# A gated long convolution and a token mixer on one core: the first channel chunk's inverse transform set aside, its gate moved behind the second chunk's spectrum stage, and the early loads reordered

## The chip, the core and the metric

The kernel runs on one core of a Trainium2 chip, in float32 (the large matrix products split each operand into a rounded half and a rest). The metric is device time in microseconds of one execution. Timed executions give a median; one further execution, taken by the hardware profiler, gives the trace that is read here.

## What is computed

Cut to what matters (S = 2048 tokens, D = 640 channels, F = 1728):

```python
sa, ca, ga, sb, cb, gb = six rows of  silu(c) @ w_mod          # (640,) @ (640, 3840)
x  = q
h  = layernorm(x) * (1 + ca) + sa
kv = causal_conv4(k, shift_k) * v                               # 4 taps, per channel
y  = causal_conv_2048(kv, ssm_k) + kv * ssm_D                   # per channel, by FFT of length 4096
x  = x + ga * (h * y)
h  = layernorm(x) * (1 + cb) + sb
x  = x + gb * (gelu(h^T @ w1 + b1) @ w2 + b2)^T                 # MLP over the token axis
```

## The kernel before

The order of all work is written by hand: each engine runs its instructions in program order, and a wait stands only where data or a buffer needs it. SyncE issues nearly all DMAs, also in program order, so a load whose destination is still in use holds up every load behind it.

The 640 channels are cut into NC = 5 chunks of DC = 128. For each chunk the long convolution runs as a transform in stages:

- `kv_ops(g)`, g = 0 to 3: the four-tap convolution and the product with v, for a quarter of the tokens, eight elementwise operations; on VectorE (one operand of the products lies in PSUM) or, with other scratch (`T_t`), on GpSimd. The result goes to X. k lies in the front and v in the rear of `T_in` (KX, VX), both chunk by chunk in the same place.
- `perm(c)`: ScalarE reorders ssm_k of the chunk from `T_aux` into P, after `perm_add(c)` has added ssm_D to its first tap. P also holds the products of the spectrum stage.
- `step1(side, t)`: first forward step (L218), side 0 from X, side 1 from P; four parts of 32 matmuls, each evicted by ScalarE (L220) into Z.
- `f2(g)`, g = 0 to 7: the spectrum stage, 64 matmuls (L233), a ScalarE copy (L237) into `T_kt`, two VectorE multiplies into P, and two sums into Y, which GpSimd does one stage later (VectorE for the last).
- `i2(r)`, r = 0, 1: first inverse step (L262), two PSUM tiles, four ScalarE evictions (L271) over the second half of Z.
- `i1(half)`: second inverse step (L282), with the constant v1, which lies in `T_v1`.
- `a1_ops(c)`: `ac`, 16 ScalarE operations (L289) that normalise the rows of q for the chunk's channels into A1 (in `T_aux`), and `po`, VectorE operations that apply the modulation rows G1 and G0.
- `gate(c, ps, half)`: VectorE multiplies A1 by the result in PSUM, GpSimd adds it to x; `spill(c)` writes x to memory.

PSUM tiles come from a ring of three (`psum()`); a fourth tile (`tap`) holds the taps and scratch of the convolution.

Before the chunk loop, chunk 0 is loaded and convolved, both its forward steps run, chunk 1 is convolved for the greater part, and q, then four of the five parts of the first half of w_mod are loaded. In chunk c's turn the stages f2 (with the rest of the convolution as `fill`, a few operations per stage), step1(0) of chunk c+1, i2, i1, gate and step1(1) of chunk c+1 follow. Chunk 0's turn is special: between these it also takes the statistics of q (L542, L543), the modulation rows (`mod_part`, L342; `mod_sum`; `mod_row`, L353) and the root of the layernorm; the parts of w_mod lie in `T_v1`, `T_aux` and P, which is why the constant v1 and ssm_k of chunk 1 are loaded only after the parts have been used:

```python
            for kk in range(4):
                mod_part(tap, kk, pl[kk])
                if kk == 1:
                    sync.dma_start(T_v1[:, 0:4096], c_v1, max_dma_last_dim=4096)
                if kk == 2:
                    load_ks(1)
            rstd(rs1, nm1, 0, 16)
```

After the five turns the token MLP follows, with large matmuls (L436, L997, L1074) that TensorE paces.

Of the kernel before, what the change touches and what calls it, by code (L numbers as in the profile page):

```python
# [12 lines left out]
ALU = mybir.AluOpType  # L13
# [36 lines left out]
def mixer_kernel(ctx: ExitStack, tc: tile.TileContext, q, k, v, shift_k, ssm_k, ssm_D, w1, b1, w2, b2, c,  # L50
# [235 lines left out]
    def a1_ops(c):  # L286

        g = lambda G: G[:, None, c * DC:(c + 1) * DC].to_broadcast([128, 16, DC])
        ac = [lambda j=j: act.activation(A1[:, j], XR(j, DC * c, DC), AF.Identity, scale=rs1[:, j:j + 1],  # L289
                                         bias=nm1[:, j:j + 1]) for j in range(16)]  # L290
        po = [lambda: TT(dve, A1, A1, g(G1), ALU.mult), lambda: TT(dve, A1, A1, g(G0), ALU.add)]
        if c in (0, NC - 1):
# [162 lines left out]
    load_ks(0, act)  # L455

# [21 lines left out]
    sync.dma_start(stg[0:13, :], dram(b1, 0, [[128, 13], [1, 128]]))  # L478
    sync.dma_start(stg[13:14, :].rearrange("p (h m) -> p h m", h=2), dram(b1, 1664, [[64, 1], [0, 2], [1, 64]]))
    sync.dma_start(stg[14:30, :], dram(b2, 0, [[128, 16], [1, 128]]))  # L480
    sync.dma_start(stg[30:35, :], dram(c, 0, [[128, 5], [1, 128]]))
# [3 lines left out]
    load_taps(2)  # L485
# [13 lines left out]
    pl = [three(t) for t in (T_v1, T_v1[:, 1920:3840], T_aux, T_aux[:, 2048:3968], P)]  # L499

    for kk in range(4):
        mod_load(0, kk, (T_v1[:, 0:1920], T_v1[:, 1920:3840], T_aux[:, 0:1920], T_aux[:, 2048:3968])[kk])
# [8 lines left out]
    for c in range(NC):  # L511
# [3 lines left out]
        for g in range(8):  # L515
# [17 lines left out]
            if c and cn is not None and g == 3:  # L533
                perm_add(cn)
# [4 lines left out]
        if c == 0:  # L539
            for j in range(16):  # L540
                for h in range(2):
                    dve.bn_stats(bst[:, j, h, :], XR(j, 320 * h, 320))  # L542
                dve.bn_aggr(mv[:, j, :], bst[:, j, 0:2, :])  # L543
        if c and c + 2 < NC:
            taps()
            if c + 3 < NC:
                load_taps(c + 3)
        if c == 0:
            mod_load(0, 4, P[:, 0:1920])
            for t in range(4):  # L550
                step1(0, t)
            ps = psum()
            pe.transpose(ps[:, 0:36], stg, ID[0:36, 0:36])
            act.activation(cols, ps[:, 0:36], AF.Copy)
            act.activation(sil, cols[:, 30:35], AF.Silu)
            i2(0)
            for kk in range(4):
                mod_part(tap, kk, pl[kk])
                if kk == 1:
                    sync.dma_start(T_v1[:, 0:4096], c_v1, max_dma_last_dim=4096)  # L560
                if kk == 2:
                    load_ks(1)
            rstd(rs1, nm1, 0, 16)
            run(ac[0:4])
            i2(1)
            mod_part(tap, 4, pl[4])
            load_k(2, 1)
            load_k(2, 2)
            load_v(2, 2)
            load_halo(2)  # L570
            load_k(2, 0)
            load_v(2, 0)
            load_v(2, 1)
            load_k(2, 3)
            load_v(2, 3)
            mod_sum(tap, T_kt[:, 0:640])
            run(ac[4:8])
            pool.tensor_scalar(PW, TR.rearrange("p (i s) -> p s i", s=4), 1.0, None, op0=ALU.mult)
            run(kv_ops(2, pool))
            for i in range(3):  # L580
                mod_row(i, T_kt[:, 0:640])
            taps()
            load_taps(3)
            perm_add(1, dve)
            perm(1)
            load_ks(2)
            run(ac[8:16])
            run(po[0:2])
            fill.extend(kv(3, ((0,), (1, 2), (3,))))
# [46 lines left out]
        for half in range(2):  # L636
            ps = i1(half)
            if c and half:
                dv(3)
            elif c:  # L640
                k0 = step1(1, 0, True)
            elif half:
                run(po[2:4])
            gate(c, ps, half)
        spill(c)
        if c:
            k0()
        for t in range(1 if c else 0, 4):
            step1(1, t)
# [3 lines left out]
        else:  # L653
            dv(11 if c else 8)
# [483 lines left out]
```

## Time and profile before

| what | value |
|---|---|
| median of three timed runs | 700.2 us (699.32 to 700.36) |
| profiled execution | 697.86 us, its span from the first to the last instruction 696.1 us |
| mean granted TensorE clock | 0.975 |
| first `f2` matmul of chunks 0, 1, 2, 3, 4 | 40.8, 115.4, 164.9, 209.2, 257.4 us |
| q | 32 loads of 160 KB, issued from 41.2 to about 68.9 us |
| w_mod, first half | 5 loads of 960 KB, issued from 68.9 to 72.5 us |
| constant v1; ssm_k of chunk 1 | 2048 KB, issued at 79.4 us; 2 loads of 512 KB, issued from 81.2 us |
| k and v, per chunk | 8 loads of 128 KB each, in packets of 256 bytes |

All numbers of the profile come from the one profiled execution. A row of the timeline reads: start, time, engine, line, operation, output and inputs, count, and in brackets the idle time ahead of it with what ended it. A row of the windows reads: stretch, length, busy time and instructions of each engine, granted clock, share of the DMA engines' time, GB/s. L59 is a helper through which all two-operand elementwise operations go, so those are told apart by their tiles.

### The profile page before, as it was taken

How to read it: one execution, taken by the hardware profiler on the slowest of the kernel's cores; microseconds unless marked ns; L12 is line 12 of the kernel's file. 1: busy time of each engine (PE TensorE's matmuls, PEld its weight loads, DVE VectorE, ACT ScalarE, POOL GpSimd, SP SyncE). 2: the span in 40 equal slices, each digit the busy share in tenths (PEclk: the TensorE clock that was granted, in tenths of full speed). 3: DMA queues.
4: the chain of work that ended last, by engine and by line, in shares of the span. 5: the costliest groups of instructions: out<-in, count | busy, mean ns of one | idle time of the engine just before them, and what ended most of it. 6: DMA issues, size and time to landing. Idle time of an engine off the chain costs nothing.

```text
span 696.1 us, 20691 instructions
## 1 busy us (share of the span) xinstructions
PE 622.0 (89%) x9099; PEld 595.8 (86%) x9099; DVE 496.1 (71%) x866; ACT 291.6 (42%) x464; POOL 128.2 (18%) x147
## 2 busy tenths in 40 slices
PE   0689777898998988888899999999999989999997
PEld 0688466788988888778899979999999989999997
DVE  6769448978979449888985741123499868888986
ACT  0444373554746536456666232232244233233331
POOL 5184018513425025000100000000000430000000
PEclk9999798999999999999999999999999999999999
DMA  9988988627443424171305604433353533466611
GB/s 183 243 227 232 381 169 178 145 43 155 91 79 111 145 64 121 59 153 32 60 1 91 121 2 99 84 61 64 110 141 104 167 121 99 121 173 172 167 44 38
DMA packets 166930, 84.37 MB, mean 121 GB/s; under 512 B 91030, under 2 KB 157368, under 8 KB 166840
## 3 DMA queue, kind: packets, MB, share of 16 engines
q1 hardware_dynamic: 162292, 81.74, 46.9%
q10 hardware_dynamic: 4548, 1.31, 1.1%
q8 instruction: 71, 1.16, 0.7%
q14 instruction: 19, 0.16, 0.1%
HBM read 72.55 MB, written 10.49 MB: 119 GB/s over the span
## 4 chain that ended last, share of the span: by engine, by line
PE 62%; DVE 17%; DMA 6%; ACT 5%; SPq 4%; issue 3%; POOL 1%; ACTq 0%; POOLq 0%; DVEq 0%
PE pst L436 20%; PE pst L997 17%; PE pst L1074 7%; PE pst L218 5%; PE pst L233 4%; PE pst L262 4%; SPq L496 3%; DVE tap L59 3%; PE pst L282 2%; DVE p L59 2%; DMA aux<-in_A_ssm_k_dram 2%; DVE kt L59 2%; DMA w<-in_const_w_dram 1%; DMA aux<-in_w_mod_dram 1%; DVE aux L59 1%
## 5 line engine op out<-in xcount | busy, mean ns | idle before, releaser
L233 PE MATMUL pst<-z,w 128*64 128x64 f32 x2560 | 79.0, 223 | 12.0 <-ACT z L220 5.7
L233 PEld LDWEIGHTS pst<-z,w 128*64 128x64 f32 x2560 | 76.8, 138 | 14.8 <-issue 7.7
L220 ACT ACTIVATE z<-pst 128x1024 f32<-128x1024 f32 x40 | 43.0, 1076 | 51.4 <-PE pst L218 51.3
L218 PE MATMUL pst<-v,x 128*64 128x128 f32 x640 | 39.6, 282 | 27.2 <-DVE x L59 24.1
L218 PEld LDWEIGHTS pst<-v,x 128*64 128x64 f32 x640 | 36.9, 142 | 28.1 <-POOL t L459 23.6
L59 DVE TENSOR_TENSOR p<-pst,kt 128x512 f32<-128x512 f32 x80 | 50.9, 680 | 12.7 <-ACT kt L237 9.3
L59 POOL TENSOR_TENSOR y<-p 128x256 f32<-128x256 f32 x72 | 51.1, 744 | 38.8 <-DVE p L59 38.6
L218 PE MATMUL pst<-v,p 128*64 128x128 f32 x640 | 39.7, 283 | 6.8 <-DVE aux L59 4.6
L997 PE MATMUL pst<-r_z,m_w 128*128 128x320 f32 x222 | 42.1, 312 | 2.2 <-DVE m_w L59 2.2
L218 PEld LDWEIGHTS pst<-v,p 128*64 128x64 f32 x640 | 37.2, 143 | 8.0 <-DVE aux L59 4.9
L262 PEld LDWEIGHTS pst<-v,y 32*128 32x128 f32 x1280 | 39.7, 194 | 3.8 <-issue 2.6
L237 ACT ACTIVATE kt<-pst 128x512 f32<-128x512 f32 x40 | 23.9, 599 | 43.7 <-PE pst L233 30.1
L262 PE MATMUL pst<-v,y 32*128 32x64 f32 x1280 | 41.6, 279 | 0.7 <-ACT z L220 0.6
L833 ACT ACTIVATE pst<-pst,sm 128x640 f32<-128x640 f32 x13 | 10.0, 767 | 75.8 <-PE pst L436 75.8
L985 ACT ACTIVATE m_w<-m_v 128x896 fp32r<-128x896 f32 x24 | 22.7, 951 | 37.0 <-PE pst L997 16.8
L997 PEld LDWEIGHTS pst<-r_z,m_w 128*128 128x128 f32 x222 | 35.2, 190 | 2.4 <-DVE m_w L59 2.4
L59 DVE TENSOR_TENSOR tap<-tap,kt 128x512 f32<-128x512 f32 x51 | 35.5, 696 | 1.3
L59 DVE TENSOR_TENSOR kt<-in,tap 128x512 f32<-128x512 f32 x51 | 34.9, 685 | 1.4
L59 POOL TENSOR_TENSOR m_p<-u_i,r_z 128x320 f32<-128x320 f32 x1 | 0.9, 882 | 183.4 <-issue 183.4
L271 ACT ACTIVATE z<-pst 128x512 f32<-128x512 f32 x38 | 20.9, 646 | 21.9 <-PE pst L262 21.9
L59 DVE TENSOR_TENSOR m_w<-m_v,m_w 128x896 fp32r<-128x896 f32 x24 | 27.9, 1164 | 2.4 <-ACT m_w L985 1.9
L436 PE MATMUL pst<-r_z,wb0b 128*128 128x320 f32 x180 | 28.2, 310 | 0.9 <-DVE u_x L59 0.9
(289 smaller groups left out, 1445.0 us busy)
## 6 DMA issues: line engine op xcount, KB each, us to landing
x<-in_B_w_dram SPq DMA_DIRECT2D x20, 512.0 KB
aux<-in_A_ssm_k_dram SPq DMA_DIRECT2D x10, 512.0 KB
in<-in_A_k_dram SPq DMA_DIRECT2D x36, 128.0 KB
in<-in_A_v_dram SPq DMA_DIRECT2D x36, 128.0 KB
m_x<-xs SPq DMA_DIRECT2D x28, 160.0 KB
out_dram<-m_x SPq DMA_DIRECT2D x28, 160.0 KB
w<-in_const_w_dram SPq DMA_DIRECT2D x2, 2048.0 KB
m_v<-in_B_w_dram SPq DMA_DIRECT2D x9, 448.0 KB
```

The costliest lines, as they stand in the source:

```text
L59: TT = lambda eng, o, a, b, op: eng.tensor_tensor(o, a, b, op=op)
L218: pe.matmul(ps[64 * ri:64 * ri + 64, o:o + 255:2], lhs, F1[:, 128 * ri:128 * ri + 128], start=True, stop=True)
L220: evac = lambda: act.activation(Z[:, side, t], ps.rearrange("p (a k e) -> p a k e", a=4, e=2), AF.Copy)
L233: pe.matmul(ps[64 * h:64 * h + 64, o:o + 64], W2[k1 // 32][:, 2 * (k1 % 32) + ri], rhs, start=True, stop=True)
L237: act.activation(kt.rearrange("p (m i) -> p m i", i=32), pv[:, :, 1], AF.Copy)
L262: pe.matmul(pp[qd // 2][:, o:o + 64], Y[p, ri, i:i + 2].rearrange("p i k -> p (i k)"), V2[p, 64 * ri:64 * ri + 64], start=ri == 0, stop=ri ...
L271: act.activation(o, i, AF.Copy)
L436: pe.matmul(ps[0:m, h, 0:320], w_.bitcast(F32R), r_[:, 320 * h:320 * h + 320].bitcast(F32R), start=first and i == 0, stop=last and i == 2)
L496: sync.dma_start(XH[j // 8][64 * b:64 * b + 64, j % 8], dram(q, (16 * b + j) * D, [[32 * D, 64], [1, D]]))
L985: act.activation(W[n][0].bitcast(F32R), A[p, w_], AF.Copy)
L997: pe.matmul(bank[n], w[:, i].bitcast(F32R), r.bitcast(F32R), start=i == 0 and k == 0, stop=i == 6 and k == 2)
L1074: pe.matmul(acc[s][:, h, 0:320], w[:, f_].bitcast(F32R), u[r + h].bitcast(F32R), start=f_ == 0 and k == 0, stop=f_ == NF - 1 and k == 2)
```

## The change

Chunk 0 is no longer gated in its own turn. The results of its `i1` are copied by ScalarE into `Y0`, which lies in v's place, and the turn of chunk 1 does the gate in four quarters (`late(n)`, rows 4n to 4n+3): the normalising of quarters 0 and 1 in the first stages of chunk 1's spectrum stage, their VectorE operations behind its end, quarters 2 and 3 among the inverse steps. The statistics of q are spread likewise: rows 0 to 7 in chunk 0's turn, 8 to 11 in chunk 1's spectrum stage, 12 to 15 behind it, with the roots by quarters (`q_root`, `q_newton`).

So that v's place is free, chunk 2 is convolved whole in chunk 0's turn; chunk 3 follows at the end of chunk 1's turn, a quarter on GpSimd and 24 operations on VectorE, 16 of them left for chunk 2's spectrum stage, spread over eight stages instead of six. Chunk 0's and 1's turns leave the common path by `continue`; those of chunks 2 to 4 keep it.

The loads stand in another order on SyncE: behind the constants of the spectrum stage ssm_k of chunk 1 and the taps of chunk 2, the constant v1, k and v of chunk 2, the first half of w_mod (now into the place of q, `T_x`), and then q, in 16 loads of two rows instead of 32 of one, which waits for the modulation's matmuls. The four small loads of b1, b2 and c go to ScalarE's queue.

The diff, cut to its core:

```diff
@@ prologue
     load_ks(0, act)
+    act.dma_start(stg[0:13, :], dram(b1, 0, [[128, 13], [1, 128]]))
...
-    load_taps(2)
...
-    for j in range(16):
-        for b in range(2):
-            sync.dma_start(XH[j // 8][64 * b:64 * b + 64, j % 8], dram(q, (16 * b + j) * D, [[32 * D, 64], [1, D]]))
+    def load_q():
+        for j in range(0, 16, 2):
+            for b in range(2):
+                sync.dma_start(XH[j // 8][64 * b:64 * b + 64, j % 8:j % 8 + 2],
+                               dram(q, (16 * b + j) * D, [[32 * D, 64], [D, 2], [1, D]]))
+    def q_stats(js):
+        for j in js:
+            for h in range(2):
+                dve.bn_stats(bst[:, j, h, :], XR(j, 320 * h, 320))
+            dve.bn_aggr(mv[:, j, :], bst[:, j, 0:2, :])
...
+    def q_root(n):
+        act.activation(tm[:, 4 * n:4 * n + 4], mv[:, 4 * n:4 * n + 4, 1], AF.Sqrt)
+    def q_newton(n):
+        o = slice(4 * n, 4 * n + 4)
+        newton(rs1[:, o], tm[:, o], mv[:, o, 1])
+        dve.scalar_tensor_tensor(nm1[:, o], mv[:, o, 0], -1.0, rs1[:, o], op0=ALU.mult, op1=ALU.mult)
+    Y0 = T_in[:, 2240:4288].rearrange("p (j d) -> p j d", j=16)
+    def late(n):
+        t = ((T_t, T_kt)[n // 2])[:, 512 * (n % 2):512 * (n % 2) + 512].rearrange("p (j d) -> p j d", j=4)
...
+        return ac, [lambda: TT(dve, t, t, g(G1), ALU.mult), lambda: TT(dve, t, t, g(G0), ALU.add),
+                    lambda: TT(dve, t, t, Y0[:, 4 * n:4 * n + 4], ALU.mult), lambda: TT(pool, x, x, t, ALU.add)]
...
+    load_ks(1)
+    load_taps(2)
+    sync.dma_start(T_v1[:, 0:4096], c_v1, max_dma_last_dim=4096)
...
@@ spectrum stage
-            if c:
+            if c > 1:
                 for f_ in ac[2 * g:2 * g + 2]:
                     f_()
+            if c == 1 and g < 2:
+                run(late(g)[0])
+            if c == 1 and g < 4:
+                q_stats(range(8 + g, 9 + g))
+            if c == 1 and 3 < g < 6:
+                run(ac[4 * g - 16:4 * g - 12])
+            if c == 1 and g == 4:
+                q_root(2)
+            if c == 1 and g == 5:
+                q_newton(2)
...
-            dv(-(-len(fill) // max((6 if c else 8) - g, 1)))
+            dv(-(-len(fill) // max((6 if c > 2 else 8) - g, 1)))
@@ chunk 0's turn, new
+            load_halo(2)
+            for g in range(4):
+                load_k(2, g)
+                load_v(2, g)
+            for kk in range(4):
+                mod_load(0, kk, T_x[kk // 2][:, 1920 * (kk % 2):1920 * (kk % 2) + 1920])
...
+            perm_add(1)
+            perm(1)
+            taps()
...
+            for t in range(4):
                 step1(0, t)
+            run(kv_ops(1, pool))
+            for g in (0, 2, 3):
+                run(kv_ops(g))
+            i2(0)
+            i2(1)
+            for half in range(2):
+                ps = i1(half)
+                act.activation(Y0[:, 8 * half:8 * half + 8].rearrange("p j (y e c) -> p e (j y) c", e=2, c=2),
+                               ps.rearrange("p (e y c) -> p e y c", e=2, c=2), AF.Copy)
+            ps = psum()
+            for kk in range(5):
+                mod_part(ps, kk, pl[kk])
+            load_q()
+            load_ks(2)
...
+            mod_sum(ps, T_kt[:, 0:640])
+            q_stats(range(4))
+            for t in range(4):
+                step1(1, t)
+                if t < 3:
+                    mod_row(t, T_kt[:, 0:640])
+            q_stats(range(4, 8))
+            for n in range(2):
+                q_root(n)
+                q_newton(n)
+            continue
@@ chunk 1's turn, new
+            run(late(0)[1] + late(1)[1])
+            q_stats(range(12, 16))
+            run(late(2)[0] + ac[8:12])
+            step1(0, 0)
+            step1(0, 1)
+            run(late(2)[1])
             i2(0)
+            q_root(3)
+            q_newton(3)
+            run(late(3)[0])
+            step1(0, 2)
+            run(late(3)[1])
             i2(1)
+            run(ac[12:16])
+            step1(0, 3)
+            run(po)
...
+            spill(0)
+            perm_add(2)
+            perm(2)
...
+            for half in range(2):
+                ps = i1(half)
+                gate(1, ps, half)
+            spill(1)
+            for t in range(4):
+                step1(1, t)
+            run(kv_ops(2, pool))
+            fill.extend(kv(4, ((0,), (1, 2), (3,))))
+            dv(8)
+            continue
```

More of the change, by code (lines that the diff above doesn't have):

```diff
@@ L531, in mixer_kernel @@
                                    dram(w1, (16 * b + g) * F, [[32 * F, 64], [1, 512]]))
[L532 to L533 removed]
+            dv(-(-len(fill) // max((6 if c > 2 else 8) - g, 1)))
+            if c > 1 and cn is not None and g == 3:
                 perm_add(cn)
@@ L538, in mixer_kernel @@
         pa_next(dve if c else pool)
[L539 to L544, printed above, removed]
+        if c > 1 and c + 2 < NC:
             taps()
@@ L548, in mixer_kernel @@
         if c == 0:
-            mod_load(0, 4, P[:, 0:1920])
+            load_halo(2)
[4 more added lines that the diff above has]
+                mod_load(0, kk, T_x[kk // 2][:, 1920 * (kk % 2):1920 * (kk % 2) + 1920])
+            for j in range(3):
+                sync.dma_start(pl[4][j], dram(w_mod, 512 * 6 * D + 640 * j, [[6 * D, 128], [1, 640]]))
+            perm_add(1)
+            perm(1)
+            taps()
@@ L550, in mixer_kernel @@
+            pool.tensor_scalar(PW, TR.rearrange("p (i s) -> p s i", s=4), 1.0, None, op0=ALU.mult)
+            load_taps(3)
             for t in range(4):
                 step1(0, t)
-            ps = psum()
-            pe.transpose(ps[:, 0:36], stg, ID[0:36, 0:36])
-            act.activation(cols, ps[:, 0:36], AF.Copy)
-            act.activation(sil, cols[:, 30:35], AF.Silu)
-            i2(0)
[L557 to L562, printed above, removed]
@@ new lines, in mixer_kernel @@
+            ps = psum()
+            for kk in range(5):
+                mod_part(ps, kk, pl[kk])
+            load_q()
+            load_ks(2)
+            load_halo(3)
+            for g in range(4):
+                load_k(3, g)
+            mod_sum(ps, T_kt[:, 0:640])
[8 more added lines that the diff above has]
+                q_newton(n)
@@ L637, in mixer_kernel @@
             ps = i1(half)
-            if c and half:
+            if half:
                 dv(3)
-            elif c:
+            else:
                 k0 = step1(1, 0, True)
-            elif half:
-                run(po[2:4])
             gate(c, ps, half)
         spill(c)
-        if c:
-            k0()
-        for t in range(1 if c else 0, 4):
+        k0()
+        for t in range(1, 4):
             step1(1, t)
```

56 lines of the change are left out of this document (23 added, 33 removed).

## The prediction

> **What bounds the kernel now.** I read the busy table of the page first, then the table of stretches, cut where the first multiply of each chunk's spectrum stage (L233, `f2`) starts, then the chain of waits inside the stretch that stands out, then the timeline.
>
> ```profile
> PE 622.0 (89%) x9099; PEld 595.8 (86%) x9099; DVE 496.1 (71%) x866; ACT 291.6 (42%) x464; POOL 128.2 (18%) x147
> 58.40:115.40 57.00, 42.18 (x841) 34.38 (x841) 36.16 (x75) 26.83 (x43) 16.73 (x14) 0.82 0.92 249
> 115.40:164.80 49.40, 43.06 (x1280) 40.98 (x1280) 40.69 (x58) 26.15 (x43) 18.21 (x20) 1.00 0.53 112
> 164.80:209.20 44.40, 42.77 (x1280) 40.99 (x1280) 39.13 (x55) 26.13 (x43) 15.40 (x18) 1.00 0.48 101
> ```
>
> TensorE is busy 89% of the span, yet the three stretches are unequal. Columns: length, then busy time (and instructions) of PE, PEld, DVE, ACT, POOL, then granted clock, DMA share, GB/s. The first has 841 matmuls against 1280, takes longer than either, at a clock of 0.82, and is the one with DMA at 0.92. After 58.4 us the first chunk's spectrum is done; the stretch holds its inverse, the modulation rows, the gate and the next chunk's forward steps. The chain of waits in it names the reason:
>
> ```profile
> 70.18 9.66 DMA aux<-in_w_mod_dram
> ...
> 81.91 15.10 DMA aux<-in_A_ssm_k_dram
> ...
> 68.00:70.00 2.00, 2.00 (x56) 2.00 (x53) 1.93 (x8) 0.34 (x2) 0.00 (x0) 0.63 0.86 229
> 76.00:78.00 2.00, 1.95 (x15) 0.47 (x12) 1.34 (x6) 0.31 (x1) 1.37 (x2) 0.50 1.04 402
> ```
>
> TensorE waits for w_mod (9.66 us), then for the second chunk's ssm_k (15.10 us); both were queued behind q on SyncE. Meanwhile the clock falls to 0.50. This is what the change is aimed at: up to 57.0 - 44.4 = 12.6 us, if the stretch became like an ordinary one.
>
> **The change, stretch by stretch.** The reordering in the prologue is nothing on the path: four small loads go to ACT's queue, which is idle then, and leave SyncE's. The spectrum stage of chunk 0 keeps its work, so it still ends at 58.4 us.
>
> *Stretch 1* (from 58.4 us). The gate, its normalising, the q statistics before them and both waits above leave it. What stays:
>
> ```profile
> 59.48 1.44 POOL L59 TENSOR_TENSOR y<-p 128x256 f32<-128x256 f32 x2 [0.85 <-DVE p L59]
> 123.61 0.78 POOL L59 TENSOR_TENSOR aux<-aux,rows 1x64 f32<-1x64 f32 x2
> 185.49 2.07 ACT L163 ACTIVATE p<-aux 128x2048 f32<-128x2048 f32 x1
> 182.35 0.69 ACT L169 ACTIVATE tap<-rows 128x256 f32<-128x256 f32 x1
> 58.46 7.21 PE L218 MATMUL pst<-v,x 128*64 128x128 f32 x128 [0.55 <-DVE x L59]
> 182.97 1.06 ACT L220 ACTIVATE z<-pst 128x1024 f32<-128x1024 f32 x1
> 184.43 3.80 PE L262 MATMUL pst<-v,y 32*128 32x64 f32 x128
> 188.26 2.23 ACT L271 ACTIVATE z<-pst 128x512 f32<-128x512 f32 x4 [0.71 <-PE pst L262]
> 196.42 2.10 PE L282 MATMUL pst<-z,v 64*64 64x64 f32 x128 [0.20 <-ACT z L271]
> 87.30 1.28 PE L342 MATMUL tap<-p,sm 128*32 128x320 f32 x12
> 90.19 1.37 PE L353 MATMUL pst<-kt,sm 1*128 1x320 f32 x12 [1.61 <-ACT kt L346]
> ```
>
> `perm(1)` now stands on ACT ahead of the forward step's evictions, and P is free only when POOL's last sums end: 60.9 + 0.8 (`perm_add`) + 2.1 + 0.7 = 64.5 us. Four evictions of 1.1 then end at 65.6, 66.6, 67.7 and 68.8. With three rotating PSUM slots the inverse's first half starts at 67.7 (before: 66.8): 3.8 to 71.5; its second half needs half of the evictions (1.1) and runs 72.6 to 76.4, evicted at 78.6; `i1` twice 2.1, to 82.8; five w_mod parts 5 x 1.28, to 89.2; the other forward step 7.2 with the three rows' 1.4, to 97.8; last eviction 98.9. VectorE's 24 convolution operations of the third chunk (0.7 each, from 64.5 to 82) and POOL's eight lie beside this; without the cover of the inverse on PE they would be in line. For half clock I add 2.0, for handovers 1.0 and for instruction fetch 1.0: 44.5 us, 12.5 less than 57.0.
>
> The 2.0 is a choice. The clock fell in 68 to 70 us with TensorE's gaps at 0.6 us and less just before it (0.55 and 0.59 in the rows here and below), and half-speed inverse work took 5.6 instead of 3.8 us. New gaps (63.9 to 65.6, 71.5 to 72.6, 76.4 to 78.6) are longer, so nothing to about 4 us is possible.
>
> ```profile
> 66.80 5.57 PE L262 MATMUL pst<-v,y 32*128 32x64 f32 x124 [0.59 <-ACT z L220]
> 80.00:90.00 10.00, 7.38 (x164) 4.74 (x163) 0.00 (x0) 4.25 (x10) 0.00 (x0) 1.00 1.07 373
> v<-in_w_mod_dram SPq DMA_DIRECT2D x2, 960.0 KB
> 100.00:110.00 10.00, 5.26 (x78) 4.78 (x76) 8.32 (x7) 4.63 (x9) 8.45 (x6) 0.80 0.72 163
> ```
>
> The loads: w_mod's 4.9 MB (five parts of 960 KB) can issue once the convolution releases v at 58.3 us; with up to 2.4 MB ahead of it that is 7.3 MB, at the 373 GB/s of 80 to 90 us some 20 us, so 78 us, needed from 82.8. q waits for the w_mod parts (it lands where they lie): 5.2 MB from 84 us take 14 us at that rate and 21 at the stretch's mean of 249, so 98 to 105 us; its last rows are needed only 23 us into stretch 2. Hidden, but see the third rival.
>
> *Stretch 2*, T from its start. Here the deferred work lands, on VectorE:
>
> ```profile
> 60.95 0.84 DVE L542 BATCH_NORM_STATS2 sm<-xa 128x6 f32<-128x320 f32 x2
> 61.83 0.21 DVE L543 BATCH_NORM_AGGREGATE sm<-sm 128x2 f32<-128x12 f32 x1
> 76.42 0.25 DVE L317 RECIPROCAL sm<-sm 128x16 f32<-128x16 f32 x1 [0.38 <-ACT sm L326]
> 77.75 0.18 DVE L331 SCALAR_TENSOR_TENSOR sm<-sm 128x16 f32<-128x16 f32 x1
> 58.71 1.29 DVE L59 TENSOR_TENSOR p<-pst,kt 128x512 f32<-128x512 f32 x2 [0.39 <-POOL y L59]
> 136.62 1.06 DVE L59 TENSOR_TENSOR y<-p 128x256 f32<-128x256 f32 x2
> 97.33 2.48 DVE L59 TENSOR_TENSOR aux<-aux,g 128x1024 f32<-128x1024 f32 x2
> 102.62 4.41 DVE L59 TENSOR_TENSOR aux<-aux,g 128x1024 f32<-128x1024 f32 x2 [1.47 <-ACT aux L289]
> 142.54 4.61 DVE L59 TENSOR_TENSOR aux<-aux,g 128x2048 f32<-128x2048 f32 x2
> 152.28 1.23 DVE L59 TENSOR_TENSOR aux<-pst,aux 128x1024 f32<-128x1024 f32 x1 [0.17 <-PE pst L282]
> 138.10 3.80 PE L262 MATMUL pst<-v,y 32*128 32x64 f32 x128
> 171.58 0.87 ACT L289 ACTIVATE aux<-xa,sm 128x128 f32<-128x128 f32 x2
> ```
>
> A row of q statistics takes about 1.03 us (0.84 and 0.21, slightly overlapped), a root's refinement 1.3 to 1.5 (first and last of its five rows), a stage's multiplies 1.29. At T = -0.4 VectorE is done with the row product and still has four q rows and two refinements, to T+6.7; then eight multiplies, four q rows, a refinement and the last sums, to T+23.6. This rate and TensorE's pace are close: the first inverse half starts near T+24 (before: 138.1 - 115.4 = 22.7). From there it is one line. The trace has no 512-wide operation of `late` (two operands in SBUF); between the 256-wide sum (0.53) and half the 1024-wide one (0.62) lies the bound without a neighbour, and half of 2.2 is the bound beside POOL. I take 0.66, nearest to the first pair, with 1.2 on top for the one set of three that runs beside a POOL sum. Six of these and 1.2: T+28.8; four q rows T+32.9; three more of `late` T+34.9; refinement T+36.4; then ACT, which stood behind it: four rows 1.75, eviction 1.1, inverse evictions 2.2, four rows 1.75, T+43.2; the undivided modulation 4.6, T+47.8; two gates 2.5, T+50.3, the first at T+49.1 releasing three forward parts of 1.8 and the last eviction 1.1: T+55.6. With handovers, 56.0: 6.6 more than 49.4. Waiting behind ACT's root and `late` rows: both evictions, hence the second inverse half; behind VectorE's refinement: `late`, modulation and gates.
>
> *Stretch 3.* Sixteen convolution operations stand in its spectrum stage instead of eight, and POOL's eight come behind its gate sums.
>
> ```profile
> 118.22 1.29 DVE L59 TENSOR_TENSOR p<-pst,kt 128x512 f32<-128x512 f32 x2 [1.98 <-ACT kt L237]
> 127.97 1.28 DVE L59 TENSOR_TENSOR p<-pst,kt 128x512 f32<-128x512 f32 x2
> 130.50 1.28 DVE L59 TENSOR_TENSOR p<-pst,kt 128x512 f32<-128x512 f32 x2
> 112.29 1.29 POOL L59 TENSOR_TENSOR x<-t,in 128x512 f32<-128x512 f32 x1
> 113.54 2.37 POOL L59 TENSOR_TENSOR xa<-xa,aux 128x1024 f32<-128x1024 f32 x1
> ```
>
> POOL gets the first gate 6.9 us ahead of the stage (49.1 of 56.0); two sums of 2.4 and eight operations of 1.3 end 8.3 us into it, and its first spectrum sum with them, so that the third multiply waits about 1.0 us. Two convolution operations and a multiply pair take 2.53 us (the distance of the last two DVE rows, with two between them). The first multiply stands 118.2 - 115.4 = 2.8 us behind the stage's start. So T+2.8, seven times 2.53, 1.28, the stall of 1.0, 1.1 for the last sums: the inverse starts at T+23.9, against 184.4 - 164.8 = 19.6 before. That is +4.3; nothing if VectorE had caught up, 5.6 at eight full operations of 0.7. Its remainder and all later chunks are unchanged, and TensorE paces what follows, so the shift passes through.
>
> Sum: -12.5 + 6.6 + 4.3 = -1.6 us. The profiled execution took 697.86 us (span 696.1), 2.3 below the median of 700.2; 696.3 for it, 698.6 for the median. A measurement of this kernel tells about 0.2% (1.4 us) from no change.
>
> **The rivals.** *Full clock, covered work* (faster). No half-clock in stretch 1 (-2.0), no collision (-1.2), handovers absorbed (-2.0): 693.4 us. For: the gaps are short. The Trainium skill ("TensorE: Matmul & The Clock Gate", What's actually happening) has the clock fall only after an idle window of about 3.4 us; by that alone the 2.0 goes, 696.6. This trace disagrees: 0.63 at 68 to 70 us behind gaps of 0.6. Against: every term was taken at an undisturbed row.
>
> *VectorE and POOL collide in stretch 2* (slower). Beside POOL the same 1024-wide operation took 2.2 instead of 1.24 us (the two rows above). If all twelve operations of `late`, where four POOL sums now fall, pay half of that difference, it is 12 x 0.5 = 6.0 instead of 1.2: 698.6 + 4.8 = 703.4 us. It decides from three colliding operations more than I allow, that is when stretch 2 exceeds 57.6 us. The Trainium skill ("SBUF — State Buffer", Who interferes with whom) makes it a lock: an operation of VectorE with two SBUF inputs waits for a whole POOL operation. The doubled row agrees. Against: in my order only one POOL sum meets `late`.
>
> *Transfers late* (slower; the change then doesn't do what it says). At 163 GB/s, the rate of 100 to 110 us, when k and v moved, 7.3 MB takes 45 us, w_mod ends at 103 and stretch 1 grows by some 15 us: 713. Against: in the rows at 373 and 402 GB/s it is w_mod and the constant that move.
>
> **How the numbers follow.** The forecast has 0.50, its own range 694.5 to 703 us: 0.25 of it faster, 0.15 same, 0.10 slower, since 1.6 lies at the bound. Full clock 0.15, collision 0.29, late transfers 0.06. Faster 0.40, same 0.15, slower 0.45. The range 691 to 707 takes in the first rival with 2 us beyond it and the second with 4 for a serial line longer than summed; it leaves out late transfers and the tails.
>
> **What would show it.** Right: stretch 1 at 42 to 47 us with no wait for w_mod or ssm_k; stretch 2 at 54 to 58, ACT waiting for VectorE's refinement; stretch 3 at 48 to 50 with VectorE ending the waits; from there on the same distances. Wrong: TensorE waiting for w_mod or q, a clock at 0.5 over more than 8 us after 60 us, stretch 2 at 50 or over 60, or a shift that does not stay constant after chunk 2.

## The result and the profile after

| what | before | after |
|---|---|---|
| median of four timed runs each, on one chip | 699.76 us (698.22 to 700.36) | 710.03 us (707.56 to 711.65) |
| ratio to before, 95% interval | | 1.0147 (1.0112 to 1.0182) |
| profiled execution, its span | 697.86, 696.1 us | 710.4, 708.6 us |
| stretch 1, 2, 3 | 57.0, 49.4, 44.4 us | 49.0, 60.9, 51.5 us |
| forecast for the three | | 44.5, 56.0, 48.7 us |

The change made the kernel 1.5% slower; the forecast was a gain of 1.6 us, with 0.45 on slower. All three stretches moved in the direction that was forecast, and each came out too long: by 4.5, 4.9 and 2.8 us.

The busy line of the page after the change, then the table of stretches cut at the same places as before (length, busy time and count of PE, PEld, DVE, ACT, POOL, granted clock, DMA share, GB/s):

```profile
PE 629.8 (89%) x9099; PEld 603.8 (85%) x9099; DVE 495.1 (70%) x881; ACT 293.8 (41%) x469; POOL 138.7 (20%) x159
...
59.20:108.20 49.00, 41.65 (x840) 34.06 (x840) 24.82 (x46) 19.42 (x23) 13.49 (x14) 0.86 0.86 236
108.20:169.10 60.90, 47.88 (x1280) 46.13 (x1280) 49.47 (x100) 34.12 (x63) 26.91 (x28) 0.86 0.63 129
169.10:220.60 51.50, 45.01 (x1280) 42.86 (x1280) 40.44 (x57) 26.27 (x43) 20.40 (x22) 0.97 0.43 91
```

The same 9099 matmuls keep TensorE busy 7.8 us longer: 4.8 of it in stretch 2 and 2.2 in stretch 3, where the granted clock is 0.86 and 0.97 instead of 1.00. TensorE's rows in time order (start, length, idle time before it and what ended it) show the rest:

```profile
59.21 5.46 PE L218 MATMUL pst<-v,x 128*64 128x128 f32 x96 [1.11 <-DVE x L59]
...
72.51 5.61 PE L262 MATMUL pst<-v,y 32*128 32x64 f32 x124 [1.02 <-ACT z L271]
79.96 5.37 PE L282 MATMUL pst<-z,v 64*64 64x64 f32 x215 [1.84 <-ACT z L271]
87.81 1.35 PE L282 MATMUL pst<-z,v 64*64 64x64 f32 x41 [2.48 <-issue]
...
97.54 1.34 PE L353 MATMUL pst<-kt,sm 1*128 1x320 f32 x4
...
116.85 13.31 PE L233 MATMUL pst<-z,w 128*64 128x64 f32 x370 [4.19 <-issue]
...
149.04 3.68 PE L218 MATMUL pst<-v,x 128*64 128x128 f32 x32 [4.24 <-ACT z L220]
...
159.66 8.34 PE L218 MATMUL pst<-v,p 128*64 128x128 f32 x120 [2.41 <-issue]
...
189.92 5.41 PE L218 MATMUL pst<-v,x 128*64 128x128 f32 x64 [4.30 <-DVE x L59]
```

No wait for w_mod or ssm_k is left, as the change intended. In its place stand, between 59 and 169 us, three stops that end with "issue": TensorE waits for nothing that the profile shows, in the middle of one loop over equal matmuls. They are 2.48, 4.19 and 2.41 us long. The modulation rows stand apart (1.34 us for each of three), stretch 2 has its wait for ACT's last eviction (4.24), and stretch 3 one for the last convolution operation (4.30).

What else ran during the stops, from the table of windows, with 75 to 84 us for the inverse steps of stretch 1 and 118 to 120 us as the time just behind the longest stop; below it, from the DMA view of 114 to 116 us, the queue that carries instructions (packets, MB, time as a share of 16 engines):

```profile
75.00:84.00 9.00, 7.16 (x208) 6.97 (x208) 6.85 (x10) 2.38 (x5) 3.01 (x3) 0.50 1.03 399
85.00:88.00 3.00, 0.52 (x32) 0.38 (x28) 0.00 (x0) 0.00 (x0) 0.00 (x0) 0.97 0.72 255
112.60:116.90 4.30, 0.11 (x4) 0.05 (x2) 4.20 (x12) 3.09 (x8) 1.56 (x3) 0.79 1.14 215
118.00:120.00 2.00, 2.00 (x42) 2.00 (x40) 0.28 (x2) 0.13 (x1) 0.18 (x1) 0.50 0.52 78
157.20:159.70 2.50, 0.09 (x4) 0.04 (x2) 2.40 (x3) 0.00 (x0) 0.62 (x1) 0.96 1.02 203
...
q8 instruction: 1, 0.02, 3.9%
```

In each stop the DMA engines are busy to 0.72 and more, and twice beyond 1.0. One packet of the instruction queue falls in each of them: at 85 to 86, 114 to 114.5 and 157.2 to 158 us. The trace has their starts at 85.36, 114.29 and 157.22 us, and TensorE goes on 2.4 to 2.6 us after each. Behind the longest stop the clock is 0.50, and so it is from 75 to 84 us.

### The profile page after: what moved, and what is told of

Its sections match the earlier page's. It is cut to its first block, busy times and chain, and to the rows that moved or that the text cites. A ratio compares the mean times of both kernels' runs of the same rounds, so it can differ in the third digit from the quotient of the medians.

```text
span 708.6 us, 20737 instructions
## 1 busy us (share of the span) xinstructions
PE 629.8 (89%) x9099; PEld 603.8 (85%) x9099; DVE 495.1 (70%) x881; ACT 293.8 (41%) x469; POOL 138.7 (20%) x159
## 4 chain that ended last, share of the span: by engine, by line
PE 63%; DVE 15%; ACT 5%; issue 4%; DMA 1%; POOL 1%; SPq 0%; DVEq 0%; ACTq 0%; POOLq 0%
PE pst L436 19%; PE pst L1075 17%; PE pst L1152 7%; PE pst L218 6%; PE pst L233 4%; PE pst L282 3%; PE pst L262 3%; DVE p L59 3%; DVE tap L59 1%; PE pst L948 1%; DVE kt L59 1%; DVE sm L548 1%; ACT z L271 1%; PE pst L342 1%; PE tap L342 1%
## 5 line engine op out<-in xcount | busy, mean ns | idle before, releaser
L233 PE MATMUL pst<-z,w 128*64 128x64 f32 x2560 | 81.1, 226 | 15.0 <-issue 8.0
L233 PEld LDWEIGHTS pst<-z,w 128*64 128x64 f32 x2560 | 79.0, 141 | 17.5 <-issue 10.8
L218 PE MATMUL pst<-v,x 128*64 128x128 f32 x640 | 42.7, 296 | 35.2 <-DVE x L59 28.6
L218 PEld LDWEIGHTS pst<-v,x 128*64 128x64 f32 x640 | 39.7, 150 | 36.2 <-POOL t L463 23.2
L237 ACT ACTIVATE kt<-pst 128x512 f32<-128x512 f32 x40 | 23.9, 596 | 43.4 <-PE pst L233 26.8
L59 DVE TENSOR_TENSOR tap<-tap,kt 128x512 f32<-128x512 f32 x48 | 33.4, 697 | 1.2
L59 DVE TENSOR_TENSOR kt<-in,tap 128x512 f32<-128x512 f32 x48 | 32.9, 686 | 1.5
L282 PEld LDWEIGHTS pst<-z,v 64*64 64x64 f32 x1280 | 23.9, 154 | 9.3 <-issue 4.5
L282 PE MATMUL pst<-z,v 64*64 64x64 f32 x1280 | 25.4, 239 | 7.0 <-issue 3.4
L271 ACT ACTIVATE z<-pst 128x512 f32<-128x512 f32 x38 | 20.8, 642 | 22.3 <-PE pst L262 22.3
```

Source lines behind the costliest of these rows:

```text
L59: TT = lambda eng, o, a, b, op: eng.tensor_tensor(o, a, b, op=op)
L218: pe.matmul(ps[64 * ri:64 * ri + 64, o:o + 255:2], lhs, F1[:, 128 * ri:128 * ri + 128], start=True, stop=True)
L233: pe.matmul(ps[64 * h:64 * h + 64, o:o + 64], W2[k1 // 32][:, 2 * (k1 % 32) + ri], rhs, start=True, stop=True)
L237: act.activation(kt.rearrange("p (m i) -> p m i", i=32), pv[:, :, 1], AF.Copy)
L271: act.activation(o, i, AF.Copy)
L282: pe.matmul(ps[64 * b:64 * b + 64, 512 * e + 64 * jj:512 * e + 64 * jj + 64], V1[p, ri, n2], T2[p, :, 32 * ri + n2], start=ri == 0, stop=r ...
```

## The experiments

Three theories, which could hold together, and a rival to each. **F**: TensorE's instructions come in blocks through the DMA engines; where these are full with a load, a block is late, TensorE stops, and the clock falls behind the stop. Rival: the stops are the loop's own, and loads have nothing to do with them. **C**: stretch 2 is the serial line of VectorE and ACT that the prediction summed. Rival: the stops and the clock set it. **X**: stretch 3 waits for the last convolution operation in front of the next forward step. Rival: it is the length of VectorE's whole list, and when the operations are issued does not matter.

The runs were timed on several chips, each with the kernel before beside it. Its median lies between 697.4 and 700.8 us on them, so the ratios can be compared with each other, and the medians only roughly.

**1. The fill of the third chunk's stage over six stages, not eight (`a_fill6`).**

```diff
-            dv(-(-len(fill) // max((6 if c > 2 else 8) - g, 1)))
+            dv(-(-len(fill) // max((6 if c else 8) - g, 1)))
```

> The changed kernel, with the rest of chunk 3's convolution spread over six spectrum stages of chunk 2 again instead of eight. Theory X: the forward step of chunk 3 stood 4.3 us behind the last convolution operation, so stretch 3 (51.5 us) shrinks by about 2 us and the whole by as much, to some 708 us. Rival: VectorE's total work sets the stage, its order does nothing: 51.5 and 710 us stay.

Measured: 706.68 us (10 runs, ratio 1.0129, 1.0095 to 1.0163). Stretch 3 by the table of windows, and the forward step that had waited 4.30:

```profile
167.40:215.30 47.90, 43.21 (x1280) 41.10 (x1280) 40.29 (x57) 26.22 (x42) 21.69 (x24) 1.00 0.50 105
...
186.49 3.72 PE L218 MATMUL pst<-v,x 128*64 128x128 f32 x64 [0.44 <-DVE p L59]
```

X holds: 47.9 us instead of 51.5, the wait 0.44 instead of 4.30. With the long wait goes the half clock behind it: 64 matmuls 3.72 us, not 5.41.

**2. The three modulation rows one right after the other (`a_rows`).**

```diff
+            for t in range(3):
+                mod_row(t, T_kt[:, 0:640])
             q_stats(range(4))
             for t in range(4):
                 step1(1, t)
-                if t < 3:
-                    mod_row(t, T_kt[:, 0:640])
```

> The changed kernel, with the three modulation rows issued one after the other ahead of the forward step, instead of one between its parts. Theory X: side by side the three rows share the array (1.37 us for all in the kernel before), apart they cost 1.34 us each; stretch 1 (49.0 us) shrinks by about 2.6 us. Rival: the forward step waits for its evictions anyway, and the rows lay in that gap: 49.0 stays.

```profile
96.03 1.37 PE L353 MATMUL pst<-kt,sm 1*128 1x320 f32 x12 [0.90 <-ACT kt L346]
```

Twelve matmuls together take 1.37 us, what four take alone. From the forward step to the next spectrum stage it is 46.8 us instead of 49.0. The total does not show it: 710.33 (ratio 1.0165, 1.0125 to 1.0205). In the profiled execution the stops in the first spectrum stage were longer (2.54 and 1.41 us instead of 1.50 and 0.40) and took the gain back.

**3. The changed kernel without the load of q (`a_noq`).**

```diff
-        for j in range(0, 16, 2):
-            for b in range(2):
-                sync.dma_start(XH[j // 8][64 * b:64 * b + 64, j % 8:j % 8 + 2], ...)
+        dve.memset(T_x[0], 0.25)
+        pool.memset(T_x[1], 0.25)
```

> The changed kernel without the load of q: constants are written in its place by VectorE and GpSimd (part left out: the load of q). Theory F (TensorE's stops in the middle of a group are its instructions arriving late while the DMA engines are full): the stop of 4.2 us at 112.7 us falls below 1 us, the half clock behind it goes, and stretch 2 falls from 60.9 to 53 to 57 us. Rival C (the serial line of late gating sets stretch 2): the stop may go, but stretch 2 stays at 59 us or more.

```profile
106.00:162.70 56.70, 46.62 (x1280) 44.47 (x1280) 49.21 (x100) 34.23 (x63) 26.76 (x27) 0.91 0.33 71
...
126.95 1.40 DVE L59 TENSOR_TENSOR t<-t,g 128x512 f32<-128x512 f32 x2
...
151.58 2.35 DVE L59 TENSOR_TENSOR aux<-pst,aux 128x1024 f32<-128x1024 f32 x2
...
153.15 8.44 PE L218 MATMUL pst<-v,p 128*64 128x128 f32 x120 [1.88 <-issue]
```

The 4.19 us stop in the second chunk's spectrum stage is gone, and stretch 2 is 4.2 us shorter, as F says. That its 56.7 us lie within 0.7 of the prediction's 56.0 is luck. `late` begins 20.9 us into the stretch (forecast 23.6) and the gates at 45.6 (forecast 47.8), and then a stop of 1.88 us and a slow forward step (120 matmuls in 8.44 us, 6.77 in run 7) take the lead back. The total was 707.87 in the one run; the fourth chunk took 53.8 us at a clock of 0.84 there, which stays unexplained.

**4. The other way about: the kernel before with two copies of 2.6 MB in the third chunk's spectrum stage (`b_burst`).**

```diff
+            if c == 2 and g in (1, 4):
+                o = 1024 * D * (g // 4)
+                act.dma_start(dram(xs2, o, [[5120, 128], [2560, 2], [1, 2560]]),
+                              dram(q, o, [[5120, 128], [2560, 2], [1, 2560]]))
```

> The kernel before, with two copies of 2.6 MB each inside memory, issued from ScalarE's queue in stages 1 and 4 of chunk 2's spectrum stage; nobody waits for them. Theory F: in the stretch from 164.8 us, which had no stop of TensorE, stops of 1 to 4 us in the middle of a group appear, and it grows from 44.4 us by 2 to 6 us. Rival: the stops belong to the changed code; no stop over 0.5 us, 44.4 us within 1 (but for 1.2 us of ScalarE's issue).

```profile
169.00:172.30 3.30, 3.30 (x116) 3.25 (x111) 3.27 (x7) 1.66 (x5) 2.21 (x4) 1.00 1.09 398
172.30:175.50 3.20, 0.03 (x3) 0.00 (x0) 3.20 (x6) 1.30 (x3) 3.05 (x7) 1.00 0.66 229
175.50:181.00 5.50, 5.49 (x127) 5.35 (x127) 2.27 (x4) 1.50 (x4) 2.08 (x3) 0.69 1.12 381
...
175.50 5.50 PE L234 MATMUL pst<-z,w 128*64 128x64 f32 x127 [3.17 <-issue]
183.28 5.28 PE L234 MATMUL pst<-z,w 128*64 128x64 f32 x122 [2.28 <-issue]
```

This stage had no stop at all before. With nothing else changed than DMA traffic that no engine waits for (and its two issues on ScalarE's queue), there are two, each followed by a run at 0.69 of the clock (127 matmuls in 5.5 us, 3.9 at full clock). The instruction packets start at 173.22 and 180.87 us, and TensorE goes on 2.3 and 2.4 us after them. The stretch grew from 44.4 to 52.7 us, the kernel to 706.01 (one run). F holds. The runs between the stops are 127 matmuls long: with their weight loads 254 instructions.

**5. The kernel before with q in two-row loads (`b_q2`)**, which the change also brought.

```diff
-    for j in range(16):
+    for j in range(0, 16, 2):
         for b in range(2):
-            sync.dma_start(XH[j // 8][64 * b:64 * b + 64, j % 8], ...)
+            sync.dma_start(XH[j // 8][64 * b:64 * b + 64, j % 8:j % 8 + 2], ...)
```

> The kernel before, with one part of the change alone: q in 16 loads of two rows instead of 32 of one. Theory L (in stretch 1 the kernel before waits for loads that stood behind q's issues): w_mod issues some 5 us earlier and stretch 1 shrinks from 57.0 us by 3 to 5 us, to some 695 us in all. Rival F: the DMA engines are then full during the first spectrum stage, TensorE's stops there grow from 0.3 to 0.5 us each to 1 to 3 us, and the gain is eaten: within 2 us of before.

```profile
40.00:58.00 18.00, 14.48 (x477) 14.20 (x476) 11.75 (x19) 5.20 (x8) 15.78 (x19) 1.00 0.90 245
...
63.08 2.19 PE L233 MATMUL pst<-z,w 128*64 128x64 f32 x36 [4.91 <-issue]
```

700.6 us (ratio 1.0027, 0.9996 to 1.0058): no gain. The loads do go faster, w_mod is issued at 62.25 instead of 68.94 us, but the DMA share in the first spectrum stage is 0.90 (0.75 before), its stops sum to 7.3 us instead of about one, and the next spectrum stage begins no earlier (116.06 against 115.45). Stretch 1 by itself did shrink, from 57.0 to 51.0 us, so L and F both hold and cancel.

**6. The kernel before with four parts of w_mod ahead of q (`b_modfirst`).** The parts are loaded and multiplied ahead of the first chunk's inverse, ssm_k and v1 follow early, and q's second half comes behind them.

```diff
+    load_q(range(0, 8, 2))
+    ...
+            load_q(range(8, 16, 2))
             for j in range(16):
                 for h in range(2):
                     dve.bn_stats(bst[:, j, h, :], XR(j, 320 * h, 320))
```

> The kernel before with its gate in place, but with the loads reordered: four parts of w_mod ahead of q, their matmuls ahead of chunk 1's forward step, so that the constant and ssm_k of chunk 1 load some 15 us earlier; q in two-row loads, its second half behind those. Theory L: the wait for ssm_k (15.1 us in the chain) goes, stretch 1 falls from 57.0 to 45 to 50 us, 688 to 694 us in all. Rival F: with the engines full the stops grow by more than 4 us and half clock follows; 696 us or more.

```profile
113.39 2.52 PE L353 MATMUL pst<-kt,sm 1*128 1x320 f32 x12 [15.48 <-ACT kt L346]
...
DVE sm L564 <- DMA xb<-in_A_q_dram: 16.9, 4, 15.0
```

718.55 us (ratio 1.0297, 1.0269 to 1.0325), far from L's 694 or less. The reordering made waits of its own. TensorE stood 5.96 us ahead of the first spectrum stage for the small loads of b1, b2 and c. Later VectorE stood 15.0 us for the second half of q; ScalarE's root waited for that, the modulation sum stood behind the root on ScalarE, and TensorE waited 15.48 us for the sum. Its first spectrum stage had stops of 1.62 and 4.97 us. What the reordering of loads alone is worth is not settled by it.

**7. The changed kernel with q in one-row loads again (`a_q1`)**: the edit of 5 the other way round.

> The changed kernel, with q in 32 one-row loads as before. Theory F: issued at 0.6 us per 160 KB, q leaves the engines room; the stop of 4.2 us in chunk 1's spectrum stage falls to 1 us or less and stretch 2 from 60.9 to 55 to 58 us, unless q's rows now come too late for the statistics (a wait of VectorE for q would show it). Rival C (serial line): stretch 2 stays at 60 us or more with no wait for q.

```profile
109.20:113.60 4.40, 4.40 (x142) 4.26 (x143) 4.03 (x19) 2.77 (x6) 0.00 (x0) 1.00 0.97 248
109.20:163.90 54.70, 45.22 (x1282) 42.96 (x1282) 48.86 (x100) 34.21 (x63) 24.86 (x26) 0.94 0.64 134
...
114.37 8.28 PE L233 MATMUL pst<-z,w 128*64 128x64 f32 x242 [0.77 <-issue]
...
155.95 6.77 PE L218 MATMUL pst<-v,p 128*64 128x128 f32 x120 [1.74 <-issue]
```

The same stretch of the spectrum stage, up to the stop, with two-row loads:

```profile
108.20:112.60 4.40, 4.35 (x142) 4.27 (x143) 4.02 (x19) 2.76 (x6) 0.00 (x0) 1.00 1.03 233
```

705.69 us (ratio 1.0122, 1.0092 to 1.0152). The stop is 0.77 us instead of 4.19, stretch 2 54.7 instead of 60.9. F holds with one part of the change undone, but not by the DMA share: up to the stop this is 0.97 here and 1.03 there. What differs is when the instruction packet starts, counted from the stage's first matmul: 1.1 us without q (run 3), 2.5 here, 6.0 with two-row loads. In all five traces of the changed kernel with two-row loads it is 5.9 to 6.1 us, in the four with one-row loads 1.7 to 2.5.

**8. The changed kernel without eight of the twelve VectorE operations of `late` (`a_nolate`).**

```diff
-        return ac, [lambda: TT(dve, t, t, g(G1), ALU.mult), lambda: TT(dve, t, t, g(G0), ALU.add),
-                    lambda: TT(dve, t, t, Y0[:, 4 * n:4 * n + 4], ALU.mult), ...
+        return ac, [lambda: TT(dve, t, t, Y0[:, 4 * n:4 * n + 4], ALU.mult), ...
```

> The changed kernel without the two modulation steps of the late quarters, 8 of their 12 VectorE operations (part left out: the modulation of chunk 0). Theory C (the late gate lies in one line on VectorE and ScalarE): stretch 2 falls by 5 to 7 us (8 times 0.7, plus what they lose beside GpSimd). Rival: VectorE's late work lies beside waits of TensorE that stay; under 2 us.

Stretch 2 took 55.9 us instead of 60.9 with its stop of 4.37 us still there, the kernel 703.33 (one run). C holds too: 5.0 us less, the lower end of what it forecast, so this stretch paid both, the stop and the line.

**9 and 10. The edits together: one-row q and six-stage fill (`a_fq`), and with them the rows side by side (`a_all`).**

> The changed kernel with two edits at once: q in 32 one-row loads, and the third chunk's spectrum stage filled over six stages instead of eight. Theory (three separate losses that add: TensorE's stops on late instructions under full DMA engines, the modulation rows, the wait of the third chunk's forward step for its last convolution operation): 710.0 - 4.3 - 3.6 = about 702, stretch 2 at 54 to 56, stretch 3 at 47 to 50; still 2 to 5 us behind the kernel before, since the serial line of stretch 2 is untouched. Rival (the stops only move: what is won in one stage comes back as a stop in another): 705 to 707.

> The same two edits and the three modulation rows issued one right after the other. Theory: 2.2 less in stretch 1 (46 to 47 us from forward step to forward step), about 700 in all, level with the kernel before. Rival (stops in the first spectrum stage eat the 2.2, as in the run with the rows alone): as without the rows, 702 or more.

702.79 us (10 runs, ratio 1.003, 0.9999 to 1.006) and 700.66 us (10 runs, ratio 0.9998, 0.9957 to 1.0039). Stretches 2 and 3 of the second:

```profile
109.90:164.60 54.70, 44.18 (x1282) 42.38 (x1282) 46.97 (x91) 33.90 (x63) 25.52 (x26) 0.97 0.63 128
164.60:212.10 47.50, 43.38 (x1280) 41.37 (x1280) 40.35 (x57) 26.21 (x42) 21.71 (x24) 1.00 0.49 105
```

Run 9 met its forecast in stretch 2 and stretch 3 (55.0 and 47.7 us) and in all. Run 10 met its total, but not where it was expected: stretch 1 took 51.2 us at a clock of 0.80, longer than the 49.0 of the changed kernel, so what the rows side by side are worth is shown by run 2 alone. That the losses are separate and simply add is not shown either: by their ratios the fill and the one-row loads alone were worth 0.18 and 0.25%, together 1.17%, and each ratio is uncertain by 0.3%. With three edits that leave the change's idea alone the loss is gone (ratio 1.0147 before the edits, 0.9998 with them), and the kernel is level with the one before, not ahead.

**11 and 12. The q statistics four rows earlier, on the changed kernel (`a_only_stats`) and on the one of 10 (`a_stats`).**

```diff
+            q_stats(range(4))
             mod_sum(ps, T_kt[:, 0:640])
-            q_stats(range(4))
...
             q_stats(range(4, 8))
+            q_stats(range(8, 12))
...
-                q_stats(range(8 + g, 9 + g))
+                q_stats(range(12 + g, 13 + g))
...
+                q_root(3)
+                q_newton(3)
...
-            q_stats(range(12, 16))
...
-            q_root(3)
-            q_newton(3)
```

> The changed kernel with the q statistics four rows earlier and nothing else: rows 0 to 3 ahead of the modulation rows (VectorE idles there), rows 8 to 11 ahead of the second chunk's spectrum stage, rows 12 to 15 in that stage, both remaining roots and refinements in it too. Theory (the second stretch is VectorE's and ACT's serial line): four rows (4.1) and one refinement with ACT's wait (3.7) leave the line behind the spectrum stage, so stretch 2 is 4 to 6 us shorter than 60.9, 704 to 706 us in all, with the stop on late instructions in that stage still there. Rival (the stretch is set by TensorE's stops and the half clock): stretch 2 within 2 us of 60.9, 709 to 711.

> The same shift of the q statistics on top of the three edits that gave 700.7 us (q in one-row loads, six-stage fill, modulation rows one after the other). Theory (the losses are separate and add): stretch 2 49 to 52 us instead of 54.7, 695 to 698 us, 0.5% faster than the kernel before. Rival (VectorE's place in line is not what ends stretch 2 any more, or the freed time comes back as a wait in stretch 3): 700 to 701, level with the kernel before.

```profile
109.70:166.00 56.30, 46.77 (x1280) 44.92 (x1280) 48.67 (x99) 33.56 (x63) 25.97 (x27) 0.91 0.66 135
...
186.79 6.50 PE L218 MATMUL pst<-v,x 128*64 128x128 f32 x64 [4.30 <-DVE x L59]
```

On the changed kernel stretch 2 became 4.6 us shorter, as C says, but the time was 709.08 us (ratio 1.0133, 1.0076 to 1.0191), as the rival says: in the profiled execution the next stage again waited 4.30 us for the convolution and then ran at half clock (6.50 us for 64 matmuls), and the first spectrum stage had stops of 1.43 and 3.06 us.

```profile
110.50:163.70 53.20, 44.88 (x1280) 42.48 (x1280) 45.25 (x86) 33.68 (x63) 26.86 (x27) 0.97 0.66 140
...
116.29 1.24 DVE L59 TENSOR_TENSOR p<-pst,kt 128x512 f32<-128x512 f32 x2
...
151.26 2.89 PE L282 MATMUL pst<-z,v 64*64 64x64 f32 x120 [2.54 <-issue]
```

On the kernel of 10 it brought 1.5 us in the stretch and, as the rival says, nothing in all: 701.46 us (12 runs, ratio 1.002, 0.9989 to 1.0051). VectorE's first multiply came 5.8 us into the stage instead of 4.3, behind the statistics moved ahead of it, and a stop of 2.54 us appeared in the second inverse step. No version beat the kernel before.

## Why the prediction was wrong

**Stretch 1, forecast 44.5, measured 49.0.** The chain was right: `perm(1)` first, four evictions, the inverse halves, five parts, the forward step, and no wait for a load. Three terms were mis-sized, by some 6 us together; the handovers and a slightly earlier inverse gave the rest back. The modulation rows were taken at 1.4 us, the row of the kernel before, where twelve matmuls stand together; apart they cost 3 x 1.34 = 4.0, which is 2.6 more (run 2 got 2.2 back). "For instruction fetch 1.0" was 2.48 in one stop. The half clock, put at 2.0, cost 4.3: it showed where it was chosen to show, 5.61 us for the second half of the inverse against 3.8, and went on in `i1`, 6.72 us (5.37 and 1.35) against 4.2.

**Stretch 2, forecast 56.0, measured 60.9.** The middle of the serial line was right: from the first operation of `late` to the gates 24.2 us were forecast and 24.7 measured, and the sign listed for it is there: ACT waits for VectorE's refinement.

```profile
133.06 1.41 DVE L59 TENSOR_TENSOR t<-t,g 128x512 f32<-128x512 f32 x2
...
135.11 2.36 DVE L59 TENSOR_TENSOR t<-t,g 128x512 f32<-128x512 f32 x2
...
142.34 1.41 DVE L59 TENSOR_TENSOR kt<-kt,g 128x512 f32<-128x512 f32 x2
...
146.40 1.65 ACT L526 ACTIVATE kt<-xb,sm 128x128 f32<-128x128 f32 x4 [3.72 <-DVE sm L517]
...
157.78 2.36 DVE L59 TENSOR_TENSOR aux<-pst,aux 128x1024 f32<-128x1024 f32 x2
```

Two operations of `late` took 1.41 us alone (forecast 1.32) and 2.36 beside POOL's sum. That collision costs 0.95; two more lie outside `late`, 0.94 in the refinement (one operation took 1.11 us instead of 0.17) and 0.5 in the undivided modulation (5.12 instead of 4.6). Together they are 2.4 us, twice the 1.2 allowed, and the collision rival with its price of 6.0 did not come about. The Trainium skill ("SBUF — State Buffer", Who interferes with whom) calls it a lock, and these rows agree.

The step that failed is a missing term: the prediction allowed for late instructions in stretch 1 only, at 1.0, and here two stops, of 4.19 and 2.41 us, stood on the path, with half clock from 117 to 122 us. Counted from the stretch's start, VectorE was ready for `late` at T+24.8. Without the first stop it would have been T+20.9, as in run 3. The forecast had T+23.6: it priced the list ahead of this 2.7 too long (the first two refinements took 0.9 us each, not 1.3 to 1.5, and the row product ended earlier), so one error hid part of the other, and that was luck. The second stop and the slow forward step behind it (120 matmuls in 8.34 us, 6.77 in run 7) made the part from the gates on 11.4 us long instead of 8.2.

The cause is in the change itself. The prediction put q's load down as hidden, which for the data it is: VectorE did not wait for it in stretch 2. But it was issued from 91.5 us, not 84, and moved at 225 to 233 GB/s, so that it still ran in the spectrum stage, and there the instructions came late. Run 7 changes nothing but the form of these loads, and run 4 makes such stops from nothing.

**Stretch 3, forecast 48.7, measured 51.5.** The prediction counted VectorE's list to the first inverse step at T+23.9 (measured T+26.1) and let the inverse follow at once. But half of the next chunk's forward step stands between, and needs the last convolution operation, which eight-stage filling issues at the very end of the stage. So the step that failed here is an overlap: the forward step was taken as done beside VectorE's list. It began at T+20.8 and ran for 5.41 us, 1.7 of them by half clock (3.72 in run 1). The stall of 1.0 for POOL did not show (384 matmuls without a gap). Run 1 took 3.6 us out by issuing the same operations earlier.

**The clock.** The prediction chose the trace's half clock behind short gaps over the rule of the Trainium skill ("TensorE: Matmul & The Clock Gate", What's actually happening), which wants an idle window of about 3.4 us. Half speed did come behind shorter stops: 0.69 behind one of 3.17 us, and 5.61 us instead of 3.8 behind a gap of 1.02. But the length of a gap does not decide it, as rows of the changed kernel and of run 4 show (in run 4 the lines of the kernel stand one higher):

```profile
135.04 3.79 PE L262 MATMUL pst<-v,y 32*128 32x64 f32 x124 [1.02 <-ACT z L220]
...
66.51 3.79 PE L263 MATMUL pst<-v,y 32*128 32x64 f32 x124 [0.58 <-ACT z L221]
```

In the first, an inverse half ran at full speed behind the same gap of 1.02 us. The second is the very half of the kernel before that the prediction read, 5.57 us behind 0.59 there. So the row on which the 2.0 rested could have come out the other way in another execution; what sets the clock here stays open. Rival "full clock" was wrong in its first term.

**What the signs told.** Of those named beforehand, "stretch 2 over 60" and a clock of 0.5 over more than 8 us came, stretch 1 left its range of 42 to 47, and the shift did not stay constant. The excess of the three stretches goes back to late instructions with the half clock behind them, rows apart and one wait. With edits against each of these (run 10) the ratio went from 1.0147 to 0.9998, although stops and half clock did not vanish. So the change without them seems to be worth about nothing, as the forecast of -1.6 us nearly said; a kernel without any such stop was not run.

**Open.** The stops in the first spectrum stage differ between executions and kernels, from about 0.3 to 5.0 us, with much the same work around them. They took back the gains of runs 2 and 5, and part of those of 11 and 12. Each follows the start of its instruction packet; why the packet comes at such different times there was not found.

## What to carry to other kernels

A load that nobody waits for is not free: while it runs, the blocks of instructions that a busy engine needs can come late. So try such a load in smaller pieces or in another stage, and read "issue" rows together with the packets of the instruction queue; the DMA share alone did not tell the stop of 0.77 us from that of 4.19. When deferred work goes behind another chunk's stage, sum that stage's serial line and then look at which instruction behind it is queued for the last of the deferred operations. Small matmuls that ran side by side are priced as a group; the three modulation rows, moved apart, cost 1.34 us each and 1.37 together.

## What the hardware showed unexpectedly

- TensorE's program arrives in packets of 16 KB, as the page's part on queues has it for the changed kernel (packets, MB, share):

```profile
q8 instruction: 71, 1.16, 0.7%
```

  Its 9099 matmuls and as many weight loads make 256 instructions for each of the 71 packets. Where stops follow each other in one loop, 127 matmuls with their 127 weight loads lie between them, or 254, and in seven of the kernels above a stop stands at the same matmul, behind the 142nd of the second chunk's spectrum stage. In the traces of all fourteen kernels, 89 stops of 0.2 us or more between 38 and 225 us end with "issue", and every one of them ends 1.2 to 1.7 us after the end of an instruction packet. The Trainium skill ("Runtime: NRT & Kernel Launch", Instruction fetch mechanics) has blocks of 16 KiB or 256 instructions, fetched through a DMA queue and mostly hidden; the sizes agree, and most packets are hidden here too: of some 30 in that time 4 to 11 show as a stop, but these reach 4.97 us, at a DMA share of 1.03.
- The same 5.2 MB in 32 loads of one row each gave a stop of 0.77 us, in 16 loads of two rows one of 4.19, at shares of 0.97 and 1.03 up to the stop. Whether it is the larger pieces that hold up the instruction packet, or how far ahead of the transfer they were issued, was not tried.
- A wait of 4.3 us in front of a forward step costs more than itself: behind it 64 matmuls took 5.41 and 6.50 us, 3.72 without it.
